# Retention and SwiGLU on one core: the later segments' retention in half chunks of 64 tokens with a state between them

## Chip, cores and metric

The kernel runs on one core of a Trainium2 chip, in float32. The metric is the device time of one execution in microseconds (us). Before the change three runs gave 666.65, 667.48 and 673.64 us, median 667.48.

TensorE is the matrix engine (PE in the profile, PEld its weight loads), VectorE is DVE, ScalarE ACT, GpSimd POOL, and SyncE (SP) issues nearly all DMAs. A bank is one of the eight [128, 512] accumulators that TensorE writes.

## Reference

A retention block is followed by a feed-forward block. Retention, for batch 4, 8 heads, 768 tokens and head size 64, with gamma = 1 - 2^(-5-head) and scale 1/8:

```python
for t in range(S):
    state = gamma * state + outer(k[:, :, t], v[:, :, t])     # 64 x 64 per head
    y[:, :, t] = scale * (q[:, :, t] @ state)
x = y.transpose(0, 2, 1, 3).reshape(B * S, H * D)             # 3072 x 512
out = (silu(x @ w_gate) * (x @ w_val)) @ w_out                # d_ff = 1536
```

The token recurrence can be cut into chunks. Within a chunk y is (q k^T with a decay mask) v, to which (q scaled by gamma^(position+1)) times the state before the chunk is added; the state after the chunk is the old state times gamma^length plus (k scaled by gamma^(what is left of the chunk))^T v. A chunk of 128 tokens has a 128x128 score matrix for each head, of which the lower triangle counts: two diagonal 64x64 blocks and one off-diagonal 64x64 block.

## The kernel before

**Segments and stages.** The 24 chunks of 128 tokens (six in each sequence) are worked in four segments of six chunks: three consecutive chunks from each of two sequences. Segments 0 and 2 begin at the start of a sequence, segments 1 and 3 in the middle. The first stage (to 143.78 us) does segment 0's retention in the older way, loads the weights, converts and splits them, writes them back to DRAM, and multiplies segment 0 by the up weights; its order is written out by hand, in `START` (L299) and `beside` (L307), one letter an action. Then come, in turn, a down stage of one segment (`down_stage`, L955) and an up stage of the next (`up3`, L873), and a last down stage.

A down stage is 72 slots, n = 6 f + b: for each of the 12 slices f of d_ff, the six token tiles. A slot is three matmuls of 128x512 (`down`, L916 and L919), the three parts into which each float32 operand is split so that the products keep their precision; they add to banks 0 to 5. In an up stage each f has seven products (a Strassen-like scheme on 2x2 blocks) of six matmuls.

**Retention between the slots.** Segment n + 1's retention is done in the down stage of segment n, in three pairs: pair p is chunk p of the segment in both sequences. Four heads' pairs of rows fill the 128 partitions, so all its matmuls work on quarters of the array, and four calls of `mm` (L550) in succession hit the four quarters. The parts of a pair are (L944 to L951): scores of head pairs 0 and 1 ("s", g = 0; `scores_of`, L555), scores of head pairs 2 and 3 (g = 1), what each chunk adds to its own bank ("m", `mix_own`, L608: `old`, L581, the old state times the queries, and `low`, L589), the rest of both ("o", `mix_other`, L619: `high`, L598, and `old`), and the new state ("t", `state2`, L651). They use banks 6 and 7, one after another; only the first pair's first score part also takes two banks that the down stage has not begun yet. Each part stands ahead of a slot (`PARTS`; pairs start at slots 2, 22 and 41).

Side work goes with each part. DVE multiplies scores by the decay mask into `tmp` (`decayed`, L571 and L573), scales one of the pair's two queries (`scale_q2`, L624; POOL scales the other, L627), and reads one column of both banks between the two mix parts (`fence`, L614 and L617), so that the other half is written only after the first is complete. ACT scales the keys (`scale_k2`, L631 and L638: eight instructions of 128x64 a chunk; POOL does one chunk of the last pair, L635) and decays the old state (`decay2`, L645 and L649); DVE adds the new sums to it (`keep_state`, L660; a copy on ACT, L663, where a sequence starts). ACT brings the finished y out of the banks (`bring_y`, L803 and L804, eight a pair). Then x is prepared for the up stage (`make_x`, L822): four sums on DVE (L80), and three splits of three steps, `far_a` (ACT, L772), `far_b` (DVE, L80 or L775), `far_c` (DVE, L778), `far_d` (ACT, L784).

Beside it runs the split of the down stage's own operand h, item f, due before slot 6 f (`h_split`, L896): `near_a` on ACT (L763), `near_b` (DVE, L766), `near_c` (DVE, L80; POOL, L769, in the up stages). SP brings the down weights (`w_load`, L909), heads (`load_pair`, L537, into five places of the tile `loads` by `HOME`, L515; `LOADS`, L952, says at which slot) and the first up weights (`load_unit`, L841; `UNITS`, L953).

**What sets the order.** Nothing is scheduled by a compiler. Each action is put down with a planned time (`at`, L120), and `run` (L123) issues all in the order of those times; the offsets stand in the table `WHEN`, and the planned cost of a part in `COST` (L951). Every engine works strictly in the order in which it was given its instructions, and waits on semaphores for what an instruction needs.

Of the kernel before, what the change touches and what calls it, by code (L numbers as in the profile page):

```python
# [17 lines left out]
P = 128  # L18
# [31 lines left out]
def tile_retnet_swiglu(  # L50
# [203 lines left out]
    def sums_t(piece, parts=range(3)):  # L254
# [30 lines left out]
        "L": lambda n: load_side(n // 2, n % 2), "h": lambda n: high_side(n),  # L285
# [6 lines left out]
    def do(order):  # L292
# [29 lines left out]
        t4 F18:2 U22:4 Z8 M8 C11 P0 | c20 Z16 a20 k5 | F18:3 Z18 T11:0 c19 C19 | a21 b20  # L322
# [30 lines left out]
        ('h', 6): (-7.31, -2.68, -1.02),  # L353
# [148 lines left out]
    def mix(c):  # L502
        vn, a = chunks[c][2], att.pop(c)
        y, own = y_parts(c)
        for k, (n, i, to) in enumerate(own):
# [7 lines left out]

    spots = [loads[:, ts(i, 512)] for i in range(10)]
    HOME = (2, 3, 4, 0, 1, 2, 3, 4, 0, 1, 4, 0)  # L515
    blocks = [loads[:, ds(i, UNIT)] for i in (2048, 2048 + UNIT, 0)]
    side = [t.rearrange("p (i t) -> p i t", i=2)
            for t in (tab[:, : 2 * TA], kept_vk.rearrange("p a b -> p (a b)")[:, : 2 * TA])]
    kdec_b = tab[:, ds(2 * TA, H)]
    half = [ds(0, D), ds(D, D)]  # L520
# [3 lines left out]
    def load_side(g, m):  # L524
        cols = decays[:, MASK0:QDEC0].rearrange("p (i g t) -> p i g t", i=2, g=2)[:, :, g]
        nc.sync.dma_start(out=side[g][half[m], :, : 2 * P], in_=cols[half[0]])
        if g == 0:
            nc.sync.dma_start(out=kdec_b[half[m]], in_=decays[half[1 - m], ds(KDEC0, H)])

    def high_side(g):  # L530

        low, high = (side[g][:, :, c].rearrange("p i (n t) -> p i n t", n=2)
                     for c in (ds(0, 2 * P), ds(2 * P, P)))
        for i in range(2):
            copy(high[:, i], low[:, i, :, :D])

    def load_pair(s, n):  # L537
        p, w = divmod(n, 4)
        w = (0, 1, 2, 3)[w]
        own = [spots[2 * HOME[n] + i] for i in range(2)]  # L540
        given.setdefault(p, {})[w] = own
        for i in range(2):
            src = (k_t, q_t, v_n, k_n)[w][seg_chunks(s)[2 * p + i]]
            if w < 2 or i == 0:
                nc.sync.dma_start(out=own[i], in_=src)
            else:
                for m in half:
                    nc.sync.dma_start(out=own[i][m], in_=src[half[m is half[0]]])
# [4 lines left out]
    score_banks = {}  # L553

    def scores_of(p, g, own=(R0, R0 + 1)):  # L555
        score_banks[p, g] = own = [banks[i] for i in own]
        kt, qt = ([pairs(t) for t in given[p][w]] for w in range(2))
        for b in range(2):
            for m in range(2):
                for r in range(2):  # L560
                    x, n = half[r], 2 * g + b
                    mm(own[r][half[m], ts(b, P)], kt[m][x, n, half[0]],
                       qt[m][x, n], b == 0)
        for b in range(2):
            for m in range(2):
                for r in range(2):
                    x, n = half[r], 2 * g + b
                    mm(own[r][half[m], ds(2 * P + D * b, D)],
                       kt[1 - m][x, n, half[1]], qt[1 - m][x, n, half[1]])

    def decayed(p, g, i):  # L571
        att[p, g, i] = tmp[:, ts(2 * g + i, TA)]
        tt(att[p, g, i], score_banks[p, g][i][:, :TA], side[g][:, i], op=mul)  # L573
# [7 lines left out]
    def old(s, p, other):  # L581
        for b in range(2):
            for h in range(2):
                for r in range(2):
                    c, n = (1 - r if other else r), 2 * h + b
                    mm(y_of(n, r, c), state_of(seg_chunks(s)[2 * p + c], 1)[half[r], n],
                       pairs(given[p][1][c])[half[r], n], b == 0 and not other)

    def low(p, first):  # L589
        for i in range(2):  # L590
            for b in range(2):
                for h in range(2):
                    for r in range(2):
                        n = 2 * h + b
                        mm(y_of(n, i, r), given[p][2][r][half[r], ts(2 * n + i, D)],
                           att[p, h, i][half[r], ts(b, P)], first and i == b == 0)

    def high(p):  # L598
        for i in range(2):
            for b in range(2):  # L600
                for h in range(2):
                    for r in range(2):
                        n = 2 * h + b
                        mm(y_of(n, i, 1 - r, half[1]),
                           given[p][2][1 - r][half[r], ts(2 * n + i, D)],
                           att[p, h, i][half[r], ds(2 * P + D * b, D)])

    def mix_own(s, p):  # L608
        ci = seg_chunks(s)[2 * p] % NCK
        if ci:  # L610
            old(s, p, False)
        low(p, ci == 0)
# [6 lines left out]
    def mix_other(s, p):  # L619
        high(p)  # L620
        if seg_chunks(s)[2 * p] % NCK:
            old(s, p, True)

    def scale_q2(p, i):  # L624
        t = pairs(given[p][1][i])
        if i:
            pool(t, t, qdec, op=mul)  # L627
        else:
            both(t, t, qdec, mul)

    def scale_k2(p, i):  # L631
        kd = given[p][3][i].rearrange("p (h d) -> p h d", h=H)
        dec = kdec_b if i else kdec
        if p == 2 and i == 0:
            pool(kd, kd, dec[:, :, None].to_broadcast([P, H, D]), op=mul)  # L635
            return
        for h in range(H):
# [477 lines left out]
```

## Time and profile before

| | us |
|---|---|
| median of three runs | 667.48 |
| the profiled execution | 665.43 |
| its span (first to last instruction) | 663.6 |
| first stage | 0 to 143.78 |
| down stage of segment 0, retention of segment 1 | 143.78 to 209.92 |
| up stage of segment 1 | 209.92 to 299.13 |
| down stage of segment 1, retention of segment 2 | 299.13 to 365.88 |
| down stage of segment 2, retention of segment 3 | 455.06 to 521.20 |
| last down stage begins | 610.0 |

The granted TensorE clock is 0.999 of full speed over the span, and 141.32 MB go over the DMA queues. Lines of the page start with a source line of the kernel, an engine and an operation with its tiles. The chain is followed back from the last instruction, at each step to what released it, and is given here in order of time: start in us, duration, engine, what it did and how many instructions. A timeline gives the same for one engine, with the idle time ahead of an instruction and what ended it in square brackets. Two matmuls of the trace belong to each float32 call on quarters.

### The profile page before, as it was taken

What the parts mean: (1) busy time and instruction counts of PE and PEld (TensorE: products, weight loads), DVE (VectorE), ACT (ScalarE), POOL (GpSimd) and SP (SyncE); (2) the same over time, 40 slices, a digit from 0 to 9 for tenths busy, and PEclk for the clock granted to TensorE, in tenths of its full rate; (3) what the DMA queues carried; (4) which work ended last, traced back from release to release, by engine and by line L of the source; (5) the groups of instructions that cost most, each with busy time, mean ns of one, the idle gap of its engine ahead of it and who ended that gap; (6) DMA issues with size and microseconds to landing.
All of it is one profiled execution on the core that took longest, in us unless ns stands there. A gap on an engine that the chain in (4) does not pass through costs nothing.

```text
span 663.6 us, 12350 instructions
## 1 busy us (share of the span) xinstructions
PE 652.2 (98%) x4712; PEld 546.0 (82%) x4712; DVE 463.1 (70%) x742; ACT 386.2 (58%) x792; POOL 252.3 (38%) x165
## 2 busy tenths in 40 slices
PE   7998999999999999999999999999999999999997
PEld 6754555567778999997777999998777999999886
DVE  4767989896768767675778666667776776668541
ACT  2688887755837555555648655555574655654221
POOL 1444557730104655640112655661000656652000
PEclk9999999999999999999999999999999999999999
DMA  9899799868665534456784533365776444323554
GB/s 325 293 387 333 258 401 396 331 248 263 210 219 216 198 112 128 159 190 207 239 261 161 206 117 142 107 215 191 229 230 229 154 178 150 112 87 112 190 191 142
DMA packets 48459, 141.32 MB, mean 213 GB/s; under 512 B 4752, under 2 KB 17808, under 8 KB 48400
## 3 DMA queue, kind: packets, MB, share of 16 engines
q1 hardware_dynamic: 47968, 139.88, 60.6%
q8 instruction: 37, 0.61, 0.4%
q10 hardware_dynamic: 432, 0.66, 0.3%
q14 instruction: 22, 0.18, 0.1%
HBM read 113.78 MB, written 26.74 MB: 212 GB/s over the span
## 4 chain that ended last, share of the span: by engine, by line
PE 84%; DMA 8%; DVE 2%; ACT 2%; issue 1%; SPq 1%; POOL 1%; ACTq 0%; POOLq 0%; DVEq 0%
PE bank L869 39%; PE bank L919 31%; PE bank L551 7%; PE bank L698 7%; DMA rawp<-in_w_gate_dram 2%; DMA loads<-in_w_out_dram 1%; DMA hT<-in_v_n_dram 1%; DMA wdnt<-oitem 1%; SPq L194 1%; DMA rawp<-in_w_out_dram 1%; DMA hT<-in_k_n_dram 1%; DMA hT<-in_k_t_dram 1%; POOL first L237 1%; ACT rawp L224 0%; ACT bank L221 0%
## 5 line engine op out<-in xcount | busy, mean ns | idle before, releaser
L869 PE MATMUL bank<-x,gitem 128*128 128x384 f32 x1296 | 231.3, 335 | 0.0
L869 PEld LDWEIGHTS bank<-x,gitem 128*128 128x128 f32 x1296 | 225.8, 188 | 0.5
L919 PE MATMUL bank<-oitem,gitem 128*128 128x512 f32 x864 | 214.0, 401 | 0.2 <-DVE hT L887 0.2
L919 PEld LDWEIGHTS bank<-oitem,gitem 128*128 128x128 f32 x864 | 159.0, 188 | 40.9 <-issue 2.9
L769 POOL TENSOR_TENSOR gitem<-gitem 128x768 fp32r<-128x768 f32 x72 | 138.7, 1946 | 113.3 <-DVE gitem L766 107.1
L698 PE MATMUL bank<-first 128*128 128x384 f32 x336 | 110.7, 489 | 2.8 <-ACT tmp L719 1.4
L698 PEld LDWEIGHTS bank<-first 128*128 128x128 f32 x336 | 62.8, 190 | 48.8 <-ACT tmp L735 2.9
L763 ACT ACTIVATE gitem<-loads 128x768 fp32r<-128x768 f32 x72 | 58.0, 840 | 36.3 <-issue 29.4
L627 POOL TENSOR_TENSOR loads<-loads,tab 128x512 f32<-128x512 f32 x8 | 12.7, 1592 | 141.5 <-PE bank L551 141.5
L766 DVE SCALAR_TENSOR_TENSOR gitem<-gitem,loads 128x768 fp32r<-128x768 f32 x72 | 65.8, 954 | 0.0
L763 ACT ACTIVATE gitem<-hT 128x768 fp32r<-128x768 f32 x48 | 40.1, 839 | 38.7 <-PE bank L919 25.2
L766 DVE SCALAR_TENSOR_TENSOR gitem<-gitem,hT 128x768 fp32r<-128x768 f32 x48 | 45.5, 952 | 18.1 <-ACT gitem L763 18.0
L237 POOL TENSOR_TENSOR first<-first,rawp 128x1024 int32<-128x1024 int32 (+1 forms) x21 | 41.0, 1959 | 30.4 <-ACT rawp L224 12.4
L80 DVE SCALAR_TENSOR_TENSOR gitem<-gitem 128x768 fp32r<-128x768 f32 x48 | 46.0, 964 | 0.9
L885 ACT COPY tmp<-bank 128x384 f32<-128x384 f32 x36 | 17.2, 479 | 46.1 <-PE bank L869 42.9
L869 PE MATMUL bank<-x,oitem 128*128 128x384 f32 x216 | 43.8, 338 | 0.0
L804 ACT COPY chunk_x<-bank 64x256 f32<-64x256 f32 x72 | 25.6, 368 | 30.7 <-PE bank L551 29.9
L769 POOL TENSOR_TENSOR oitem<-oitem 128x256 fp32r<-128x256 f32 x36 | 28.2, 783 | 29.8 <-DVE oitem L766 27.9
L888 DVE TENSOR_TENSOR hT<-hT,bank 128x384 f32<-128x384 f32 x36 | 19.9, 553 | 27.0 <-ACT bank L888 27.0
L886 DVE TENSOR_TENSOR hT<-bank,tmp 128x384 f32<-128x384 f32 x36 | 20.1, 558 | 26.6 <-PE bank L869 26.6
L869 PEld LDWEIGHTS bank<-x,oitem 128*128 128x128 f32 x216 | 38.0, 188 | 0.0
L884 DVE TENSOR_TENSOR tmp<-bank,tmp 128x384 f32<-128x384 f32 x36 | 20.1, 557 | 18.9 <-PE bank L869 18.8
(99 smaller groups left out, 720.8 us busy)
## 6 DMA issues: line engine op xcount, KB each, us to landing
oitem<-wdnt SPq DMA_DIRECT2D x45, 768.0 KB, 4.4
loads<-wup SPq DMA_DIRECT2D x36, 896.0 KB, 4.9
wup<-first SPq DMA_DIRECT2D x12, 896.0 KB, 8.7
wdnt<-oitem SPq DMA_DIRECT2D x12, 768.0 KB, 4.7
rawp<-in_w_gate_dram SPq DMA_DIRECT2D x12, 512.0 KB, 8.2
rawp<-in_w_val_dram SPq DMA_DIRECT2D x12, 512.0 KB, 7.6
out_dram<-chunk_x SPq DMA_DIRECT2D x23, 256.0 KB, 2.2
loads<-in_q_t_dram SPq DMA_DIRECT2D x18, 256.0 KB, 4.5
```

Of the source, the lines that this page charges most:

```text
L80: stt(o, x, 1.0, y, op0=mul, op1=op)
L237: pool(d.bitcast(I32), d.bitcast(I32), lo.bitcast(I32), op=add)
L551: nc.tensor.matmul(o, a, b, start=start, stop=True, skip_group_check=True)
L698: nc.tensor.matmul(o, w[:, slot, k], a[:, KH - 1 - k], start=(start and k == 0), stop=(stop and k == KH - 1), skip_group_check=True)
L763: act(o[0], x, AF.Copy, scale=CUT / FAR)
L766: stt(o[1], f32(o[0]), -FAR, x, op0=mul, op1=add)
L769: op(o[2], f32(o[0]), f32(o[1]), op=add)
L804: copy(cx[half[i], ds(2 * h, 2), c], y_both(h, i, c))
L869: nc.tensor.matmul(o, w[:, a, k], xs_of[s][:, a, OP[p], KH - 1 - k], start=start and a == k == 0, stop=a == 2 and k == KH - 1, skip_group_ ...
L884: steps = (lambda: copy(p1, x), lambda: tt(c11, z, p1, op=add), lambda: act(gate, c11, AF.Silu, scale=ONE), lambda: copy(u2, x), lambda: c ...
L886: lambda: copy(p5, wb), lambda: tt(h1, x, p5, op=add),
L919: nc.tensor.matmul(banks[tok], hs[f][:, a, ds(i * TH + u * P, P)], wo[f][:, a], start=f == a == 0, stop=f == NF - 1 and a == 2, skip_group ...
```

## The change

The retention of segments 1 to 3 is done in half chunks of 64 tokens, with a state between the two halves of a chunk.

- Scores: only the diagonal 64x64 blocks, 32 calls of 64x64x64 a pair in one part; the masks shrink to one tile of 2x256 columns a partition (`side`), and are applied by one instruction a bank (`decayed`).
- The off-diagonal block is replaced by a middle state, `mids`: old state times gamma^64 (`decay2`, with `g64`, made once by the new `decay_64`) plus the sum over the first half; even pairs have it in `tab`, pair 1 in `tmp`. The second half's queries meet `mids` in `old`, the first half's the state before. `state2` makes the sums of both halves in two banks, DVE adds the first to `mids` and ACT copies the second (`keep_state`); `next_state` is four DVE instructions, new = mid x g64 + second sum. The last chunk of a sequence needs only the first sum.
- Queries are scaled in two halves (`scale_q2`), both by the first 64 columns of the table; keys in eight instructions of 128x2x64 for both chunks of a pair (`scale_k2`).
- A pair's parts are states "t", scores "s", own half "m", other half "o". The first pair's states and scores are one part ahead of slot 2, the states in two banks of the down stage. The state parts of pairs 1 and 2 stand ahead of slots 19 and 39, and so before their scores, not after their mix.
- Keys are scaled and states decayed earlier: the first pair's before the down stage (in the later up stages one head at a time), pair 1's keys at slot 16, pair 2's at slot 30. Head loads are put in another order with other places (`PLACES`): untransposed keys and values first, queries last; pair 2's queries take the place of its keys. Pair 0's queries of segment 1 are loaded in the first stage (`P3`).
- The planned times of h item 6 are earlier, and the planned cost of a part is 1.2.

Most lines that both kernels have stand on the same line in both (the slots' matmuls at L919 for one). In the changed kernel the others are: `mm` L553/554, `scores_of` L556, `decayed` L568, `old` L576, `own_half` L587, `fence` L603, `scale_q2` L609 (POOL L613), `scale_k2` L621, `state2` L639, `keep_state` L655/657 (DVE) and L659 (ACT), `next_state` L665. The core of the diff:

```diff
-        t4 F18:2 U22:4 Z8 M8 C11 P0 | c20 Z16 a20 k5 | F18:3 Z18 T11:0 c19 C19 | a21 b20
+        t4 F18:2 U22:4 Z8 M8 C11 P0 P3 | c20 Z16 a20 k5 | F18:3 Z18 T11:0 c19 C19 | a21 b20
...
-        ('h', 6): (-7.31, -2.68, -1.02),
+        ('h', 6): (-8.3, -4.0, -2.6),
...
-    HOME = (2, 3, 4, 0, 1, 2, 3, 4, 0, 1, 4, 0)
+    PLACES = [(0, 0, 4), (0, 2, 3), (0, 3, 2), (0, 1, 0), (1, 3, 1), (1, 2, 2), (1, 0, 4), (1, 1, 3),
+              (2, 3, 0), (2, 2, 1), (2, 0, 4), (2, 1, 0)]
...
+    side = kept_vk.rearrange("p a b -> p (a b)")[:, : 2 * NP * D].rearrange("p (i m) -> p i m", i=2)
     kdec_b = tab[:, ds(2 * TA, H)]
+    g64 = tab[:, ds(2 * TA + H, NP)]
+    mids = [t.rearrange("p (c n e) -> p c n e", c=2, n=NP)
+            for t in (tab[:, : 2 * NP * D], tmp[:, ds(4 * NP * D, 2 * NP * D)])]
...
+    def decay_64(n):
+        if n == 0:
+            act(g64, qdec[:, :, D - 1], AF.Copy, scale=8.0)
...
-    score_banks = {}
-
-    def scores_of(p, g, own=(R0, R0 + 1)):
-        score_banks[p, g] = own = [banks[i] for i in own]
+    def scores_of(p):
         kt, qt = ([pairs(t) for t in given[p][w]] for w in range(2))
-        for b in range(2):
-            for m in range(2):
-                for r in range(2):
-                    x, n = half[r], 2 * g + b
-                    mm(own[r][half[m], ts(b, P)], kt[m][x, n, half[0]],
-                       qt[m][x, n], b == 0)
-        for b in range(2):
-            for m in range(2):
-                for r in range(2):
-                    x, n = half[r], 2 * g + b
-                    mm(own[r][half[m], ds(2 * P + D * b, D)],
-                       kt[1 - m][x, n, half[1]], qt[1 - m][x, n, half[1]])
-
-    def decayed(p, g, i):
-        att[p, g, i] = tmp[:, ts(2 * g + i, TA)]
-        tt(att[p, g, i], score_banks[p, g][i][:, :TA], side[g][:, i], op=mul)
+        for c in range(2):
+            for n in range(NP):
+                for e in range(2):
+                    for r in range(2):
+                        mm(banks[R0 + r][half[c ^ e], ts(c * NP + n, D)],
+                           kt[c][half[r], n, half[e]], qt[c][half[r], n, half[e]], c == n == 0)
+
+    def decayed(p, i):
+        att[p, i] = tmp[:, ts(i, 2 * NP * D)]
+        o, x = (t.rearrange("p (c m) -> p c m", c=2) for t in (att[p, i], banks[R0 + i]))
+        tt(o, x, side[:, i][:, None, :].to_broadcast([P, 2, NP * D]), op=mul)
...
-    def low(p, first):
+        cs = seg_chunks(s)[2 * p : 2 * p + 2]
+        for e in range(int(cs[0] % NCK == 0), 2):
+            for b in range(2):
+                for h in range(2):
+                    for r in range(2):
+                        c, n = (1 - r if other else r), 2 * h + b
+                        st = mids[p % 2][:, c] if e else state_of(cs[c], 1)
+                        mm(y_of(n, r, c, half[e]), st[half[r], n],
+                           pairs(given[p][1][c])[half[r], n, half[e]])
+
+    def own_half(p, e):
         for i in range(2):
             for b in range(2):
                 for h in range(2):
                     for r in range(2):
-                        n = 2 * h + b
-                        mm(y_of(n, i, r), given[p][2][r][half[r], ts(2 * n + i, D)],
-                           att[p, h, i][half[r], ts(b, P)], first and i == b == 0)
-
-    def high(p):
-        for i in range(2):
-            for b in range(2):
-                for h in range(2):
-                    for r in range(2):
-                        n = 2 * h + b
-                        mm(y_of(n, i, 1 - r, half[1]),
-                           given[p][2][1 - r][half[r], ts(2 * n + i, D)],
-                           att[p, h, i][half[r], ds(2 * P + D * b, D)])
+                        c, n = r ^ e, 2 * h + b
+                        mm(y_of(n, i, c, half[e]), given[p][2][c][half[r], ts(2 * n + i, D)],
+                           att[p, i][half[r], ts(c * NP + n, D)], e == i == b == 0)
 
     def mix_own(s, p):
-        ci = seg_chunks(s)[2 * p] % NCK
-        if ci:
-            old(s, p, False)
-        low(p, ci == 0)
+        own_half(p, 0)
+        old(s, p, False)
...
-        high(p)
-        if seg_chunks(s)[2 * p] % NCK:
-            old(s, p, True)
+        own_half(p, 1)
+        old(s, p, True)
 
     def scale_q2(p, i):
-        t = pairs(given[p][1][i])
-        if i:
-            pool(t, t, qdec, op=mul)
-        else:
-            both(t, t, qdec, mul)
-
-    def scale_k2(p, i):
-        kd = given[p][3][i].rearrange("p (h d) -> p h d", h=H)
-        dec = kdec_b if i else kdec
-        if p == 2 and i == 0:
-            pool(kd, kd, dec[:, :, None].to_broadcast([P, H, D]), op=mul)
-            return
-        for h in range(H):
-            act(kd[:, h], kd[:, h], AF.Copy, scale=dec[:, ds(h, 1)])
-
-    def new_states(s, p):
+        t = given[p][1][i].rearrange("p (n e t) -> p n e t", n=NP, e=2)
+        for e in range(2):
+            if i:
+                pool(t[:, :, e], t[:, :, e], qdec[:, :, :D], op=mul)
+            else:
+                both(t[:, :, e], t[:, :, e], qdec[:, :, :D], mul)
+
+    def scale_k2(p, heads=range(H)):
+        home = [h for q, w, h in PLACES if (q, w) == (p, 3)][0]
+        kd = loads[:, ts(home, 2 * DM)].rearrange("p (c h d) -> p c h d", c=2, h=H)
+        for h in heads:
+            act(kd[:, :, h], kd[:, :, h], AF.Copy, scale=kdec_b[:, ds(h, 1)])
+
+    def place_of(s, p):
         ci = seg_chunks(s)[2 * p] % NCK
-        new, was = (states[:, (ci + o) % 2] for o in range(2))
-        return ci, new, was, banks[R0].rearrange("p (c n e) -> p c n e", c=2, n=NP)
+        return ci, states[:, ci % 2], states[:, (ci + 1) % 2], mids[p % 2]
 
     def decay2(s, p):
-        ci, new, was, st = new_states(s, p)
+        ci, new, was, mid = place_of(s, p)
         if ci:
             for n in range(NP):
-                act(new[:, :, n], was[:, :, n], AF.Copy, scale=gdec[:, ds(n, 1)])
-
-    def state2(s, p):
-        ci, new, was, st = new_states(s, p)
+                act(mid[:, :, n], was[:, :, n], AF.Copy, scale=g64[:, ds(n, 1)])
...
+    def state2(s, p, own=(R0, R0 + 1)):
+        state_banks[p] = own
+        ci, seen = place_of(s, p)[0], set()
         for c in range(2):
             vn, kd = given[p][2][c], given[p][3][c]
             for n in range(NP):
-                for i in range(2):
-                    h = ts(2 * n + i, D)
-                    mm(st[half[i], c, n], kd[:, h], vn[:, h], c == n == 0)
-
-    def keep_state(s, p):
-        ci, new, was, st = new_states(s, p)
+                for e in range(2 - (ci == NCK - 1)):
+                    for i in range(2):
+                        r, h = c ^ e, ts(2 * n + i, D)
+                        mm(sum_of(p, c, e)[half[i], n], kd[half[r], h], vn[half[r], h],
+                           (r, i) not in seen)
+                        seen.add((r, i))
+
+    def keep_state(s, p, c):
+        ci, new, was, mid = place_of(s, p)
         if ci == 0:
-            copy(new, st)
+            nc.vector.tensor_copy(mid[:, c], sum_of(p, c, 0))
         else:
-            tt(new, new, st, op=add)
+            tt(mid[:, c], mid[:, c], sum_of(p, c, 0), op=add)
+        if ci < NCK - 1:
+            copy(new[:, c], sum_of(p, c, 1))
+
+    def next_state(s, p):
+        ci, new, was, mid = place_of(s, p)
+        if ci < NCK - 1:
+            for n in range(NP):
+                stt(new[:, :, n], mid[:, :, n], g64[:, ds(n, 1)], new[:, :, n], op0=mul, op1=add)
...
-    CYCLE = [("s", 0, 0), ("s", 1, 4), ("m", 0, 9), ("o", 0, 12), ("t", 0, 16)]
-    STARTS = (2, 22, 41)
-    PARTS = {}
-    for p, b in enumerate(STARTS):
-        for what, g, n in CYCLE:
-            PARTS[b + n] = what, p, g
-    del PARTS[STARTS[0] + 4]
-    COST = {"s": 1.0, "m": 1.3, "o": 1.1, "t": 0.8}
-    LOADS = {5: 7, 6: 15, 7: 19, 8: 19, 9: 27, 10: 39, 11: 46}
+    PARTS = {2: "s0", 8: "m0", 11: "o0", 19: "t1", 23: "s1", 29: "m1", 32: "o1",
+             39: "t2", 45: "s2", 50: "m2", 53: "o2"}
+    SCALES = {1: 16, 2: 30}
+    COST = 1.2
+    LOADS = {5: 4, 6: 5, 7: 12, 8: 13, 9: 20, 10: 25, 11: 38}
...
+                what, p = PARTS[n][0], int(PARTS[n][1])
                 ci = seg_chunks(nxt)[2 * p] % NCK
-                d = t + COST[what] + 0.1
+                if n == 2 or what == "t":
+                    at(t, state2, nxt, p, ((4, 5) if s else (4, 3)) if n == 2 else (R0, R0 + 1))
+                    t += COST
+                    for c in range(2):
+                        at(t + 0.1 * (1 + c), keep_state, nxt, p, c)
+                    at(t + 2.5, next_state, nxt, p)
+                d = t + COST
...
+                    at(t, scores_of, p)
                    for i in range(2):
+                        at(d + 0.3 + 0.1 * i, decayed, p, i)
+                        at(d + 0.35 + 0.1 * i, scale_q2, p, i)
...
+                    if p < 2:
+                        at(d + 4.0, decay2, nxt, p + 1)
...
+            for p, h in SCALES.items():
+                at(slot_at[h], scale_k2, p)
...
-    for n in range(3, 5):
-        at(end + 1.0 + n, load_pair, 1, n)
+    at(end + 5.0, load_pair, 1, 4)
+    at(end - 1.0, decay2, 1, 0)
+    at(end - 1.0, scale_k2, 0)
...
-                at(t - (18, 13, 12, 5, 4)[n], load_pair, s + 1, n)
+                at(t - (13, 12, 18, 5, 4)[n], load_pair, s + 1, n)
+            for h in range(H):
+                at(t - 12 + 1.0 * h, scale_k2, 0, [h])
+            at(t - 8.0, decay2, s + 1, 0)
```

## Prediction

> **What bounds the kernel now.** I read the first part of the page, then its chain by line, then the chain in order of time through the first two reworked down stages, then the ACT and DVE timelines around the same places, last the landings of the head loads.
>
> ```profile
> PE 652.2 (98%) x4712; PEld 546.0 (82%) x4712; DVE 463.1 (70%) x742; ACT 386.2 (58%) x792; POOL 252.3 (38%) x165
> PE bank L869 39%; PE bank L919 31%; PE bank L551 7%; PE bank L698 7%; DMA rawp<-in_w_gate_dram 2%; DMA loads<-in_w_out_dram 1%; DMA hT<-in_v_n_dram 1%; DMA wdnt<-oitem 1%; SPq L194 1%; DMA rawp<-in_w_out_dram 1%; DMA hT<-in_k_n_dram 1%; DMA hT<-in_k_t_dram 1%; POOL first L237 1%; ACT rawp L224 0%; ACT bank L221 0%
> ```
>
> TensorE carries the end: from 127 us on the chain hardly leaves it. L551 is the retention of the later segments, 7% of the span. A matmul saved there shortens the span unless a wait takes its place.
>
> ```profile
> 143.78 1.50 PE bank L551 x64
> 145.28 6.49 PE bank L919 x27
> 151.77 1.47 PE bank L551 x48
> 153.24 2.30 PE bank L919 x9
> 155.54 1.06 PE bank L551 x48
> 156.61 3.00 PE bank L919 x12
> 159.60 1.08 PE bank L551 x32
> 160.68 3.00 PE bank L919 x12
> 163.68 0.83 PE bank L551 x32
> ...
> 307.13 1.03 PE bank L551 x32
> 308.16 2.30 PE bank L919 x9
> 310.46 0.62 PE bank L551 x32
> ```
>
> Each call of `mm` is two matmuls of the trace. Four calls that hit the four 64x64 quarters of the array run together; I call four such matmuls a quad. 310.46 is 8 quads of 64 columns, 307.13 is 8 of 128 columns, 155.54 is 8 of 64 and 4 of 128, 151.77 is 12 of 128. 1.06 - 0.62 gives 0.11 a quad of 128; then 1.03 = 8 x 0.11 + 0.15, so a part has 0.15 fixed, and 0.62 gives 0.0585 a quad of 64. Check: 143.78 (8 + 8 quads) comes to 1.50, 163.68 (4 + 4) to 0.82. The down matmuls behind a part follow n x 0.233 + 0.20 (2.30, 3.00), so each part also costs 0.20 by interrupting them.
>
> ```profile
> 156.66 3.04 ACT L804 COPY chunk_x<-bank 64x256 f32<-64x256 f32 x8 [2.79 <-PE bank L551]
> ...
> 169.09 1.06 ACT L784 ACTIVATE x<-x 128x1024 fp32r<-128x1024 f32 x1
> 170.06 0.83 ACT L763 ACTIVATE gitem<-hT 128x768 fp32r<-128x768 f32 x1
> 170.79 1.27 ACT L649 ACTIVATE states<-states,tab 128x128 f32<-128x128 f32 x4
> 171.96 2.01 ACT L638 ACTIVATE loads<-loads,tab 128x64 f32<-128x64 f32 x8
> 173.87 0.83 ACT L763 ACTIVATE gitem<-hT 128x768 fp32r<-128x768 f32 x1
> ```
>
> ```profile
> 167.84 1.22 DVE L778 SCALAR_TENSOR_TENSOR x<-x 128x1024 fp32r<-128x1024 f32 x1
> ...
> 173.56 0.42 DVE L617 COPY warm<-bank 128x1 f32<-128x1 f32 x2 [2.79 <-PE bank L551]
> 174.74 1.83 DVE L766 SCALAR_TENSOR_TENSOR gitem<-gitem,hT 128x768 fp32r<-128x768 f32 x2 [0.76 <-ACT gitem L763]
> 176.48 1.82 DVE L80 SCALAR_TENSOR_TENSOR gitem<-gitem 128x768 fp32r<-128x768 f32 x2
> ```
>
> The weights' side engines run in order, and hand work to each other: the wide x split (L778) frees L784, behind it stand the near_a of h items 6 and 7 (L763), and DVE takes both near_b (174.74) before both near_c (176.48). Item 6 is done near 177.4; its first use, slot 36, has its third matmul at 176.87 + 0.20 + 2 x 0.70 + 0.47, about 178.9 (176.87 is the end of the other half at slot 34; two slots of three matmuls lie between). That is 1.5 us of slack, no more.
>
> **Part by part: TensorE.** Removed: the full 128-column score, old and low/high products (24 quads of 128 columns and 16 of 64 a pair) and the 128-row state part. Added: scores, own halves, old and states, all 64x64x64, 16 quads each. A part becomes 16 x 0.0585 + 0.15 = 1.09; the joint first part (states and scores, 32 quads) 2.03. In the segments that begin inside a sequence the last pair keeps only the middle state: its calls use two quarters at a time, as the old state part does (1.08). So segments 1 and 3: 2.03 + 9 x 1.09 + 1.08 = 12.92 in 11 parts, against 14.57 (the chain's thirteen L551 pieces from 143.78 to 196.43 added) in 13: 1.65 + 2 x 0.20 = 2.05 less. Segment 2, where the first pair has no earlier state in its first half: 2.03 + 2 x 0.85 + 8 x 1.09 = 12.45 in 11, against 14.97 in 14: 2.52 + 0.60 = 3.1 less. All three: 7.2 us. The price of a quad is bounded by 0.0585 and, if a longer run of them starved, by the 128-column quad, 0.11; I take 0.0585, the same shape.
>
> **Where the cover ends.** Positions in segment 1: joint part 143.78 to 145.81, then 150.21 first mix, 154.69 end of its other half, 160.49 states of pair 1, 164.58 scores, 170.07 mix, 174.55 end of the other half. Slot 36's third matmul would be at 174.55 + 0.20 + 2.80 + 0.47 = 178.0.
> ACT starts bring_y at 154.74: 8 x 0.38 (3.04 above), then the moved key scaling of pair 1, 8 x 0.29 (the step of the 128x128 L649), L772 0.31, four decays 1.16, L772 0.54 and 0.97, near_a 0.74, L784 0.33, the new state copy 0.38: 164.5. States of pair 1 are ready: scaling ends at 160.1, 0.4 ahead of 160.49.
> DVE's second half-state add shares its bank with that copy and waits for it: 164.6. Then add 0.34, x 1.13 and 0.60, four new next_state 1.0 (no row; between 0.20, the slope of the 256 to 1024 rows, and 0.34, the 256 step), near_b 0.87, mask 0.60, two half q scalings 0.67, mask 0.60: 170.5. The mix at 170.07 waits 0.4. Behind it near_c 0.87 and L778 1.22: 172.5.
> ACT idles for that L784, then 0.97 + near_a of item 6 0.74 + key scaling of pair 2 8 x 0.29 + near_a of item 7 0.83: 177.4. DVE: near_b of item 7 0.87, near_c of item 6 0.96: 179.3. Slot 36, now at 178.4, waits 0.9. Together 1.3 us in each segment; the order is the same in all three: 3.9. With the cheaper ends (0.20, and 0.25 a scaling) it is 0.7; with isolated durations (0.42 a next_state, 0.39 a scaling) 2.5. So 2.1 to 7.5 in all, and I take 3.9.
> That wait pushes bring_y of pair 1 to 180.4, past 179.7 where the states of pair 2 would overwrite its banks; with slot 36 late they come at 181, so it costs nothing more.
>
> **Edits costed at nothing.** First key scaling and decays in segment 1 (3.8 us) go into ACT's 4.58 us wait before 143.12; that cover has 0.8 to spare. In the up stages single scalings of 0.29 stand between copies; ACT there waits for PE at nearly every copy. Before segment 3 seven stand together (2.0), bounded by 0 and 0.5 us. POOL's two half scalings (1.3 to 1.8 a whole one) end 2 us before the mix. The moved loads on SP: key rows first, queries late. Queries of pair 0 now go out beside its transposed keys near 110 us, ahead of a weight store, but SP then waits until 119.05 for DVE, so the extra transfer has 7 us. One is tight: queries of pair 2 take the place of pair 2's keys and go out only when its states end (E). Scores need the first half at E + 4.4, the second by E + 4.9; behind it on SP stand a down weight (needed 7 us later) and an up unit.
>
> ```profile
> DMA to landing us min/median/max: 2.4/3.9/9.4
> ```
>
> Pairs of query loads alone land in 3.3 to 5.5 there, so 0, with up to 4.5 us a segment at the maximum.
>
> **Sum.** 665.43 - 7.2 + 3.9 = 662.1 for the profiled execution (span 663.6). The median of the runs, 667.48, stands 2.05 above it: 667.48 - 3.3 = 664.2.
>
> **A rule against the trace.** In the row 310.46 the eight quads pass at 14.6 ns a matmul. The Trainium skill, "TensorE: Matmul & The Clock Gate", section "Wait — 56ns, not 53.3ns?", says that starts never come closer than about 25 ns however small the matmul. By that rule a quad would be an estimated 0.10, the 536 quads would cost 22 us more, and the time would be near 686. The row disagrees for calls on different quarters, and the row decides.
>
> **Rivals.**
> 1. No wait: the side engines keep up, as in 174.74 to 178.30 before. Against it: the exact queue order above. 667.48 - 7.2 = 660.3. Chance 0.19.
> 2. The opposite side: the queries of pair 2 arrive late. Place: slot 45, three times. They have about 4.6 us; each us over costs 3. From 5.7 us of landing the gain of 3.3 is gone. For it: the value loads that follow an up unit land in 6.3 to 6.7; against: these go ahead of the up unit. At 6.7: 3 x 2.1 = 6.3, 670.5; at 9.4 678.6. Chance 0.14.
> 3. Long runs of small quads starve. The longest run of 64-column quads in the trace is 8, the new ones are 16 and 32. The gain is gone from 0.0585 + 3.3 / 536 = 0.065 a quad; at 0.11, 27.6 us more, 691.8. Against: the 64 matmuls at 143.78 show no slowing. Chance 0.05.
>
> **How the numbers follow.** The forecast, waits of 0.7 to 2.5 a segment, has 0.62: 660 to 668 around 664.2. Range: 660.0 to 669.5 takes in rival 1 and the shorter half of rival 2. One per cent, 6.7 us, is about what a measurement of this kernel can tell from none: faster by more needs below 660.8, which is most of rival 1 and a little of the forecast, 0.2; slower by more is rival 3 and the far end of rival 2, 0.1; within 0.7.
>
> **What would show it.** L551 pieces of 1.09 and 2.03 and eleven a segment: TensorE right. An issue or DVE wait of about 0.9 before the third matmul of slot 36, and of 0.4 before pair 1's mix: the chain right. ACT idle for L784 some 5 us there: its link. PE waiting for in_q_t at the third scores: rival 2. Pieces longer than 1.2: rival 3. I am wrong if waits stand elsewhere, in the up stages or in the first stage's weight stores.

## The result and the profile after

The changed kernel takes 669.49 us (median of 20 runs, 668.43 to 670.85), the kernel before 667.39 (20 runs): a ratio of 1.0026, 95% interval 1.0014 to 1.0039. The forecast was 664.2, a gain of 3.3; there is a loss of 2.1. The profiled execution after took 668.43 (span 666.6), 3.0 more than the one before.

From the page: the busy time of each engine after, then the chain by engine, before and after:

```profile
PE 649.5 (97%) x5288; PEld 544.4 (82%) x5288; DVE 471.4 (71%) x774; ACT 387.1 (58%) x778; POOL 259.3 (39%) x174
```

```profile
PE 84%; DMA 8%; DVE 2%; ACT 2%; issue 1%; SPq 1%; POOL 1%; ACTq 0%; POOLq 0%; DVEq 0%
```

```profile
PE 70%; DVE 9%; ACT 8%; DMA 6%; issue 3%; POOL 3%; SPq 1%; DVEq 0%; ACTq 0%; POOLq 0%
```

TensorE's work did shrink (652.2 to 649.5), but TensorE carries less of the end: its share of the chain falls from 84% to 70%, and DVE and ACT have 17%. From the first retention part to the last down stage TensorE waited once before, 0.2 us for DVE (L887). After, its waits there are these (what it waited for, us in total, times, longest); the last is the old one:

```profile
PE bank L919 <- DVE gitem L80: 2.3, 3, 0.8
PE bank L554 <- DVE tmp L568: 2.1, 3, 0.7
PE bank L554 <- ACT states L659: 0.7, 3, 0.3
PE bank L919 <- DVE hT L887: 0.2, 1, 0.2
```

Three new stalls, each once a segment. TensorE's timeline of the first reworked stage shows where:

```profile
165.91 1.33 PE L554 MATMUL bank<-loads 64*64 64x64 f32 x64 [0.25 <-ACT states L659]
...
172.58 0.63 PE L554 MATMUL bank<-tmp,loads 64*64 64x64 f32 x27 [0.68 <-DVE tmp L568]
...
181.34 1.90 PE L919 MATMUL bank<-oitem,gitem 128*128 128x512 f32 x7 [0.77 <-DVE gitem L80]
```

They are pair 1's scores (waiting for ACT to copy the state sums out of the bank), pair 1's mix (for the masks) and the third matmul of slot 36 (for near_c of h item 6). They cost more than the idle time in brackets. Counted from the start of one run of matmuls to the start of the next, against the same runs without a stall, TensorE loses 0.48, 1.00 and 1.02 us, 2.5 a segment. Below, "idles" is the gap that the trace shows and "loses" is this larger figure.

By stage, from the first matmul of one to the first of the next (the first down stage from its first retention part):

| us | before | after | forecast of the difference | measured |
|---|---|---|---|---|
| first stage, to the first retention part | 143.71 | 144.81 | 0 | +1.10 |
| down stages with retention | 66.05, 68.15, 67.55 | 66.34, 67.87, 67.83 | -3.3 | +0.29 |
| up stages | 87.81, 87.77, 87.83 | 88.23, 88.61, 88.15 | 0 | +1.58 |
| the rest | 54.78 | 54.80 | 0 | +0.02 |

### The profile page after: what moved, and what is told of

Its sections match the earlier page's. It is cut to its first block, busy times and chain, and to the rows that moved or that the text cites. A ratio compares the mean times of both kernels' runs of the same rounds, so it can differ in the third digit from the quotient of the medians.

```text
span 666.6 us, 13548 instructions
## 1 busy us (share of the span) xinstructions
PE 649.5 (97%) x5288; PEld 544.4 (82%) x5288; DVE 471.4 (71%) x774; ACT 387.1 (58%) x778; POOL 259.3 (39%) x174
## 4 chain that ended last, share of the span: by engine, by line
PE 70%; DVE 9%; ACT 8%; DMA 6%; issue 3%; POOL 3%; SPq 1%; DVEq 0%; ACTq 0%; POOLq 0%
PE bank L869 39%; PE bank L919 16%; PE bank L698 10%; PE bank L554 4%; ACT chunk_x L804 2%; ACT loads L621 2%; DMA rawp<-in_w_gate_dram 2%; DVE gitem L766 2%; POOL gitem L769 2%; ACT gitem L763 1%; DVE gitem L80 1%; DMA wdnt<-oitem 1%; DMA hT<-in_v_n_dram 1%; DVE x L778 1%; DVE x L80 1%
## 5 line engine op out<-in xcount | busy, mean ns | idle before, releaser
L919 PE MATMUL bank<-oitem,gitem 128*128 128x512 f32 x864 | 213.0, 400 | 2.5 <-DVE gitem L80 2.3
L919 PEld LDWEIGHTS bank<-oitem,gitem 128*128 128x128 f32 x864 | 159.2, 188 | 43.0 <-DVE gitem L80 3.6
L769 POOL TENSOR_TENSOR gitem<-gitem 128x768 fp32r<-128x768 f32 x72 | 140.1, 1968 | 111.6 <-DVE gitem L766 106.4
L613 POOL TENSOR_TENSOR loads<-loads,tab 128x256 f32<-128x256 f32 x18 | 20.2, 1143 | 140.5 <-PE bank L554 140.5
L766 DVE SCALAR_TENSOR_TENSOR gitem<-gitem,loads 128x768 fp32r<-128x768 f32 x72 | 65.6, 951 | 0.0
L766 DVE SCALAR_TENSOR_TENSOR gitem<-gitem,hT 128x768 fp32r<-128x768 f32 x48 | 45.7, 952 | 27.3 <-ACT gitem L763 27.2
L80 DVE SCALAR_TENSOR_TENSOR gitem<-gitem 128x768 fp32r<-128x768 f32 x48 | 46.0, 964 | 0.9
L804 ACT COPY chunk_x<-bank 64x256 f32<-64x256 f32 x72 | 25.5, 367 | 33.1 <-PE bank L554 32.4
L784 ACT ACTIVATE x<-x 128x256 fp32r<-128x256 f32 (+2 forms) x27 | 18.8, 696 | 35.4 <-DVE x L778 35.4
L769 POOL TENSOR_TENSOR oitem<-oitem 128x256 fp32r<-128x256 f32 x36 | 27.7, 769 | 29.4 <-DVE oitem L766 26.1
L886 DVE TENSOR_TENSOR hT<-bank,tmp 128x384 f32<-128x384 f32 x36 | 20.1, 557 | 26.9 <-PE bank L869 26.9
```

Of the source, the lines that this page charges most:

```text
L80: stt(o, x, 1.0, y, op0=mul, op1=op)
L613: pool(t[:, :, e], t[:, :, e], qdec[:, :, :D], op=mul)
L766: stt(o[1], f32(o[0]), -FAR, x, op0=mul, op1=add)
L769: op(o[2], f32(o[0]), f32(o[1]), op=add)
L804: copy(cx[half[i], ds(2 * h, 2), c], y_both(h, i, c))
L886: lambda: copy(p5, wb), lambda: tt(h1, x, p5, op=add),
```

## The experiments

**What makes the new states dear.** DVE's timeline around pair 1's new states (L665), and POOL's at the same time, in the changed kernel:

```profile
167.09 0.68 DVE L778 SCALAR_TENSOR_TENSOR x<-x 128x512 fp32r<-128x512 f32 x1
167.69 2.10 DVE L665 SCALAR_TENSOR_TENSOR states<-tmp,tab,states 128x128 f32<-128x128 f32 x4
169.71 0.95 DVE L766 SCALAR_TENSOR_TENSOR gitem<-gitem,hT 128x768 fp32r<-128x768 f32 x1
```

```profile
167.34 1.78 POOL L613 TENSOR_TENSOR loads<-loads,tab 128x256 f32<-128x256 f32 x2 [18.10 <-PE bank L554]
```

Two of the four take 0.83 and 0.82 us, the other two 0.34; the slow ones end 0.15 us after POOL's two scalings of a query. The same instruction for pairs 0 and 2 takes 0.34 in all 16 cases.

```diff
-            if i:
+            if i and p != 1:
                 pool(t[:, :, e], t[:, :, e], qdec[:, :, :D], op=mul)
```

> Against the changed kernel (profiled 668.43): pair 1's second query is scaled by DVE instead of POOL, so POOL is idle while DVE makes pair 1's new states. Theory A (the four next_state cost 2.02 us instead of the 1.0 of the forecast because POOL's scaling runs beside two of them): all four take 0.26 a step, 1.05 together, and the stall before pair 1's mix falls from a lost 1.0 us to 0.2 or less. Rival B (an instruction of this kind costs 0.5 there by its operands, or waits for ACT's copy): two of the four stay above 0.8 us. The wait at slot 36 grows from 1.0 to about 1.5 by A, as DVE has 0.67 us more work behind the mask; profiled time about 1.2 us shorter by A, 2 us longer by B.

DVE's timeline, with POOL idle:

```profile
169.06 1.13 DVE L665 SCALAR_TENSOR_TENSOR states<-tmp,tab,states 128x128 f32<-128x128 f32 x4
170.11 0.95 DVE L766 SCALAR_TENSOR_TENSOR gitem<-gitem,hT 128x768 fp32r<-128x768 f32 x1
```

All twelve of them take 0.34 (0.26 from one start to the next). Theory A holds, B falls. The mix now loses only 0.04, and slot 36 idles 1.43 (loses 1.70), both as expected. The down stages are 0.3 us shorter each, 0.9 in all, where 1.2 was expected. The one run took 668.55, no less than before the edit, because its first stage was 1.4 longer; a single run shows no gain in time, and only its trace is used here.

**Taking them out of the way.**

```diff
-                    at(t + 2.5, next_state, nxt, p)
+                    at(t + (9.6 if p == 1 else 2.5), next_state, nxt, p)
```

> Pair 1's next_state is given to DVE behind the fence of pair 1's mix instead of ahead of near_b and the masks. Theory (DVE's queue holds the mix back): the masks come 1.0 to 2.0 us earlier (1.0 if POOL's scaling then slows near_b instead), the stall before the mix goes, and each segment gets 1.0 us shorter; slot 36 still waits, 0.5 to 1.0. Time 666.5 (ratio to the kernel before 0.9985). Rival (the mix waits for POOL's scaled query, or for the other mask's bank): the stall stays and the time is that of the changed kernel, 669.5.

664.25 us, ratio 0.9959 (0.9946 to 0.9971): a larger gain than expected (666.5). In DVE's timeline POOL's scaling now meets near_b (L766), which takes 1.50 instead of 0.95, and the new states are cheap behind the fence:

```profile
167.86 1.50 DVE L766 SCALAR_TENSOR_TENSOR gitem<-gitem,hT 128x768 fp32r<-128x768 f32 x1
...
173.47 1.13 DVE L665 SCALAR_TENSOR_TENSOR states<-tmp,tab,states 128x128 f32<-128x128 f32 x4
...
178.16 0.96 DVE L766 SCALAR_TENSOR_TENSOR gitem<-gitem,hT 128x768 fp32r<-128x768 f32 x1 [2.12 <-ACT gitem L763]
179.04 1.82 DVE L80 SCALAR_TENSOR_TENSOR gitem<-gitem 128x768 fp32r<-128x768 f32 x2
```

The mix's stall is gone, and slot 36 loses 0.55 instead of 1.02, because the wide L778 that ACT's chain waits for ends 1.3 us earlier, and TensorE comes only 0.8 earlier. Each down stage is 1.46 to 1.48 shorter, 4.4 in all. The last two lines still show what item 6 waits for: its near_c (L80) stands behind near_b of item 7 (L766).

**One link of slot 36 alone.**

```diff
-        ('h', 6): (-8.3, -4.0, -2.6),
+        ('h', 6): (-8.3, -4.0, -3.7),
```

> One planned time: near_c of h item 6 is put ahead of near_b of item 7 on DVE. Theory (slot 36 waits because near_c of item 6 stands behind near_b of item 7, which stands behind eight key scalings on ACT): the wait at slot 36, 1.0 us a segment, goes; the stalls before pair 1's scores (0.5) and mix (1.0) stay. Time 666.5 (ratio 0.9985). Rival (item 7 or the down weight is then late for slot 42, or near_a of item 6 itself is late): the wait moves or stays, time 668.5 to 669.5.

670.67 us, ratio 1.0047 (1.0034 to 1.0061), more than theory or rival allowed. Slot 36 has no idle time any more, but pair 2's mix, which had hardly waited, now loses 0.65 us in two segments and 2.2 in the other. TensorE reaches it 0.9 us earlier, while DVE and ACT, which bring its masks, are as late as before, and in two segments an instruction ahead of these masks meets POOL's scaling of pair 2 (188.99 to 191.71):

```profile
189.35 1.76 DVE L778 SCALAR_TENSOR_TENSOR x<-x 128x1024 fp32r<-128x1024 f32 x1
```

In the changed kernel the same instruction takes 1.22: there it starts at 189.37, ahead of POOL's scaling at 189.87, and here at 189.35, behind it. In the second segment it is pair 2's new states (L665) that meet POOL's scaling, 2.12 us for the four instead of 1.13. The first and third down stages are 0.2 shorter, the second 1.0 longer. The wait moved, as the rival has it, but to a place that the rival did not name.

**The copies that clear the bank**, on top of the late new states, and alone.

```diff
                     for c in range(2):
-                        at(t + 0.1 * (1 + c), keep_state, nxt, p, c)
+                        at(t + 0.1 * (1 + c) - (1.1 if p == 1 else 0), keep_state, nxt, p, c)
...
-        ('far', 0, 1): (4.43, 6.67, 7.61, 7.97),
+        ('far', 0, 1): (5.9, 6.67, 7.61, 7.97),
...
-        ('far', 0, 0): (4.85, 7.08, 11.35, 11.95),
+        ('far', 0, 0): (6.0, 7.08, 11.35, 11.95),
```

> On top of the late next_state: pair 1's two state copies on ACT (and DVE's adds) are given ahead of two x splits instead of behind them and near_a. Theory (the stall before pair 1's scores, a lost 0.48 us a segment, is the score part waiting for ACT's second copy to clear the bank, and the 1.4 us in which DVE waits for that copy hold back all behind it to slot 36): both that stall and the rest at slot 36 (0.55) go, each segment is 1.0 us shorter, time 661.2 against 664.25 (ratio to the kernel before 0.991). Rival (slot 36 is held by ACT's own sequence of splits and key scalings, which gets no shorter): only the first stall goes, 662.8.

662.58 us, ratio 0.9935 (0.9917 to 0.9953), nearer the rival; the interval overlaps that of the late new states alone, so that no gain in time over them is shown. In the first segment the stall before the scores is gone and slot 36 loses 0.31 instead of 0.55, but 0.41 us comes back ahead of pair 2's mix: a down weight has not landed. The second segment loses 0.78 there in the same way, and the third 1.0 in pair 0's other half, in an idle time for which the trace shows no wait. Against the late new states alone the first two down stages are 0.33 and 0.28 shorter, the third 0.25 longer; this profiled run, at 664.07, was the longest of six. The waits of TensorE, new ones only:

```profile
PE bank L919 <- DMA oitem<-wdnt: 0.7, 2, 0.5
...
PE bank L554 <- issue: 0.7, 1, 0.7
```

> Against the changed kernel, only the two copies of pair 1's state on ACT given early; next_state stays where it is, and takes its 2.02 us. Theory: the stall before pair 1's scores (0.48) goes, DVE's queue is 1.3 us earlier, so the stall before the mix falls from 1.0 to 0.2 or less, and slot 36 waits about 1.0 as before: each down stage is 1.2 to 1.5 us shorter. Rival (next_state alone decides the mix's wait): that stall stays at 1.0 or grows, 0.5 us a stage.

Alone it gave 667.79 in one run, of which only the trace is used. The stall before the scores is gone; the mix still idles 0.42 (loses 0.74), where 0.2 or less was expected, since the wide splits on ACT moved behind the copies, so that DVE is 0.8 earlier at L665 and not 1.3, and L665 still takes 2.0. The down stages are 0.17 (with 0.36 idle for a down weight), 0.76 and 0.75 shorter.

**The first stage.** Its chain of waits runs through a store of down weights (start, length, what), before:

```profile
119.42 6.03 DMA wdnt<-oitem
```

and after:

```profile
119.02 7.52 DMA wdnt<-oitem
```

```diff
-        t4 F18:2 U22:4 Z8 M8 C11 P0 P3 | c20 Z16 a20 k5 | F18:3 Z18 T11:0 c19 C19 | a21 b20
+        t4 F18:2 U22:4 Z8 M8 C11 P0 | c20 Z16 a20 k5 | F18:3 Z18 P3 T11:0 c19 C19 | a21 b20
```

> The queries of segment 1's first pair are loaded behind the third of the weight stores in the first stage instead of ahead of them. Theory C (the first stage is 1.1 us longer because 0.5 MB of queries stand in a saturated queue ahead of a weight store whose landing ends the wait): the store lands in about 6.0 us again instead of 7.5, slot 2 begins 1.1 us earlier, and the time is 668.4 (ratio 1.0010). Rival (the first stage of the one profiled run before was a lucky one): landing 7 to 7.5, no change, 669.5 (1.0026).

670.55 us, ratio 1.0045 (1.0027 to 1.0063), not faster. The queries now stood between two stores on SP, and the second, whose landing counts, went out at 122.51, 1.8 us behind the first instead of 0.4; it landed 6.46 later. The stage was 2 us late before that point already in the profiled run, the longest of eight, so its end (148.93) says little. Moved once more, behind the last of the three stores:

```diff
-            F19:0 b21 | F19:1 S20 S21 a22 a23 C20 Z17 | T11:1 F19:2 |
+            F19:0 b21 | F19:1 S20 S21 a22 a23 C20 Z17 P3 | T11:1 F19:2 |
```

> Only the queries of segment 1's first pair moved, now behind the last weight store that the first stage waits for (the earlier try had put them between two stores, ahead of the one that matters, whose issue was 1.4 us late). Theory C: that store lands in about 6.0 us instead of 7.5 to 7.8, slot 2 begins about 1.3 us earlier than the changed kernel's 144.8 to 146.2, time 668.2 (ratio 1.0012). Rival (the landing varies from run to run): 7.5 and 669.5.

```profile
119.41 5.92 DMA wdnt<-oitem
```

The store lands in 5.92, and the first part starts at 143.59. In the two kernels below that also load the queries behind it, the store lands in 6.27 and 5.99 and the part starts at 144.40 and 144.26. In the seven kernels that load the queries ahead of all three stores it lands in 7.2 to 7.8, and the part starts at 144.80 to 146.18. From the store's issue to the first part it is 24.2 to 24.5 us in these three and in the kernel before, and 25.5 to 26.1 in those seven. Theory C holds in the traces. In time, 667.83 and 1.0018 (1.0007 to 1.0028) stand below the changed kernel's 1.0026, but the intervals overlap, so that no gain is shown there.

**The up stages' start.** In the changed kernel the fifth matmul of each up stage waits for POOL's near_c (L769) and starts 0.42 us behind the fourth, not 0.17. Its chain at the first one:

```profile
208.16 3.89 POOL gitem L769
...
212.10 3.05 PE bank L869 x16
```

The removed last state part had also taken planned time (0.8 behind slot 56, also in the segments whose last pair runs no state part). Without it the splits of h item 11 and the up weights are planned ahead of x work of pair 2, and the order on DVE and ACT changes.

```diff
-            t += 3 * PASS_D
+            t += 3 * PASS_D + (0.7 if nxt and n == 56 else 0)
```

> Against the changed kernel: 0.7 us put back into the planned times behind slot 56, where the removed state part of the last pair had stood. Theory: the order of DVE and ACT ahead of an up stage is again that of the kernel before, and the wait of 0.24 us for POOL at the fourth matmul of each up stage is gone; profiled time 0.7 us shorter, the rest unchanged. Rival (the splits are late because the x work itself is longer): the wait stays.

The matmul that the expectation calls the fourth is the fifth. The up stages take 87.98, 87.96 and 87.79, 1.3 us less in all than the changed kernel's: the late matmul is gone from each, as it is in the two kernels below that put the planned time back, and in none of the other eight. A loss of 0.33 at the end of the second up stage is gone too, but two kernels without this edit do not have it either (POOL's scaling moved to DVE, and the queries between two stores). About 0.2 in each of the first two up stages is left over the kernel before. The one run took 667.50.

**All together**: late new states, early copies, queries behind the stores, planned time put back.

> Late next_state, early copies, queries behind the store, and the planned time of the removed last state part (0.7 behind slot 56) put back. Theory: 664.25 - 3.1 (the stalls of the late kernel) - 1.2 (store) - 0.7 (three up stages begin without the 0.24 us wait) = 659.3, ratio 0.988. Rivals: the store's term is noise, 660.5; a wait moves to pair 2 as it did when near_c was moved alone, 660.5 to 662.

660.25 us, ratio 0.9901 (0.9883 to 0.9919), 6.5 us faster than the kernel before beside it (666.74). The expectation was 659.3; the time is nearer to its first rival, in which the store's term is noise (660.5). Between the first retention part and the last down stage TensorE waits no more often than before the change, and the chain by engine is its own again:

```profile
PE bank L919 <- DVE hT L887: 0.3, 1, 0.3
```

```profile
PE 89%; DMA 6%; DVE 2%; issue 1%; SPq 1%; POOL 1%; ACT 0%; ACTq 0%; POOLq 0%; DVEq 0%
```

With near_c of item 6 moved as well:

> The kernel with all four moves and, on top, near_c of h item 6 ahead of near_b of item 7. In the kernel with the four moves near_c of item 6 ends at 178.64, as TensorE reaches it (178.51), which costs 0.31 us a segment. Theory (with the chain ahead of it mended, this move no longer hands its wait to pair 2): slot 36 has no wait, 0.9 us less in all, time 659.3 (ratio 0.989). Rival (the wait goes to pair 2's mix, as when it was moved alone): 660.3 or more.

660.66 us, ratio 0.9903 (0.9888 to 0.9918), no different, which is the rival's time. The 0.31 at slot 36 is gone, and the first and third down stages are 0.2 shorter, but the second is not: 0.27 us idle ahead of pair 2's mix. What is left there is too small to be told in time.

## Why the prediction was wrong

- **TensorE: right.** Parts of 1.09 and 2.02 and eleven a segment, as forecast. In the kernel with all four moves the parts take 12.74, 12.51 and 12.74 us, against 14.57, 14.77 and 14.57: 5.9 less, and 7 pieces fewer at 0.20, 7.3 together (forecast 7.2). Two small errors of the forecast nearly cancel here: the pieces of segment 2 before add up to 14.77, not 14.97, and the last pair's state part of segments 1 and 3 takes 0.91, not 1.08.
- That the time of that kernel, 660.25, is the first rival's 660.3 is partly luck. Its trace has the down stages 6.4 shorter than before, with 0.9 of the 7.3 still lost, the up stages 0.5 longer and the first stage 0.7 longer, 5.2 in all; the profiled run before, 665.43, was the fastest of 20.
- **The waits: the place right but for one, the size wrong.** Forecast 1.3 a segment, 0.4 at pair 1's mix and 0.9 at slot 36; measured 1.00, 1.02, and 0.48 before pair 1's scores: 2.5, the upper bound. The step that failed is the term "four new next_state 1.0": the four took 2.0. Beside an idle POOL they take 1.05 (first experiment), so the price of the instruction alone was right, and what was missing is that POOL scales a query at the same time. Moving them out of the way took 4.4 us off the down stages, more than the 3.6 by which their forecast was off.
- The profile before did have a row for it. DVE's scaling of a query, 128x512, took 0.68 at 147.69, after POOL's had ended (146.66), and 0.87 at 169.90, beside it (168.41 to 170.22):

```profile
147.69 0.68 DVE L80 SCALAR_TENSOR_TENSOR loads<-loads,tab 128x512 f32<-128x512 f32 x1
169.90 0.87 DVE L80 SCALAR_TENSOR_TENSOR loads<-loads,tab 128x512 f32<-128x512 f32 x1
```

```profile
145.36 1.30 POOL L627 TENSOR_TENSOR loads<-loads,tab 128x512 f32<-128x512 f32 x1 [7.74 <-PE bank L551]
168.41 1.81 POOL L627 TENSOR_TENSOR loads<-loads,tab 128x512 f32<-128x512 f32 x1 [21.76 <-PE bank L551]
```

- The Trainium skill names the cause: "SBUF — State Buffer", section "SBUF: two separate sides", has VectorE and GpSimd share a pair of ports under an exclusive lock for a whole instruction, where the DVE instruction has both inputs in SBUF and GpSimd's reads SBUF. The runs agree on which instructions are slowed: 0.82 to 0.83 against 0.34 (L665), 1.50 against 0.95 (L766), while the mask product, with one input in a bank, took 0.68 beside POOL (169.28 in the kernel with the late new states) and alone.
- **The stall before the scores.** "States of pair 1 ... 164.5" counted one copy of ACT; there are two, and the scores need both banks. It is 0.48 a segment, and gone where the copies were given earlier.
- A stall cost 0.23 to 0.32 us more than its idle time; the forecast counted idle time alone.
- **Costed at nothing, the up stages: wrong, 1.6.** About 0.25 at each start and 0.33 at the second one's end; the rest, about 0.5, has no cause shown. The cause of the first is the planned time that left with the last state part, a thing that the diff shows only as a line removed from a list of parts. The cause of the 0.33 stays open. The seven scalings ahead of segment 3 were bounded by 0.5 but are not shown to be the cause: three kinds of kernel that have them do not lose the 0.33.
- **Costed at nothing, the queries in the first stage: wrong, about 1.2.** The words "so the extra transfer has 7 us" looked at the time until SP's next store, not at what was still in the queue: the first of the three stores, issued at 111.30 before, lands only at 121.8, and the DMA engines are busy almost without a break until 124.
- The forecast had named these two places itself, under what would show it wrong: waits "in the up stages or in the first stage's weight stores".
- Rival 2 did not happen: the queries of pair 2 landed in 2.7 to 3.6 us in the changed kernel, and TensorE never waits for them. Rival 3 did not either: 128 matmuls in 2.02 us, 15.8 ns each. The rule of "TensorE: Matmul & The Clock Gate" that was weighed there, 25 ns, is not what these rows show.
- Sum for the profiled execution: 7.3 less on TensorE, 7.6 more in waits (2.5 a segment and 0.1), 1.6 more in the up stages and 1.1 in the first stage: 3.0 longer, as measured. Of the first stage's 1.1, part differs from run to run.

What stays open: an idle time of 0.41 us on DVE ahead of L886 at the end of the second up stage, with nothing that it waits for. It goes with the 0.33 above: most variants have it, and those with the planned time put back, with one scaling moved from POOL to DVE, or with the queries between two stores have not. The last of these changes only loads in the first stage, so the order on DVE cannot be the whole cause.

## What to carry to other kernels

Price a new vector instruction with what the neighbouring engine does at that moment, and look for a row of the same pair of engines side by side; a mean hides it. When a part is removed from a planned or hand-ordered schedule, its planned time goes too, and the order of everything behind it is then a change of its own. A wait that is taken away at one link only comes back at the next as long as the chain behind it is late; here the late new states, which took work off the way to the masks, paid, and the swap of two steps at slot 36 alone did not.

## What the runs showed of the hardware

- DVE instructions with two inputs in SBUF were slowed beside POOL's multiplications: four small ones in a row came out as 0.83, 0.82, 0.34, 0.34 beside two POOL instructions, and 0.34 each without them.
- In a pair of rows, which of the two started first decided who was slowed: the 128x1024 split (L778) took 1.22 where it started 0.50 us ahead of POOL's scaling (189.37 in the changed kernel; POOL's 128x256 took 1.32), and 1.76 where it started 0.36 behind it (189.35 with near_c moved; POOL's took 1.04).
- A TensorE stall of 0.25 us idle cost 0.48, one of 0.77 cost 1.02, one of 1.43 cost 1.70.
- Half a megabyte of loads ahead of a store in a full queue delayed its landing from 5.9 to 6.3 us (four kernels) to 7.2 to 7.8 us (seven).
